# Fused attention and two expert layers: a batch's values in six tiles, loaded once

## The chip, the cores and the metric

One core of one Trainium2 chip runs the whole program. The metric is the time on the device in microseconds (us); the median over several executions counts. One further execution was recorded by the profiler, and every duration below comes from that one.

## The reference, cut to what matters

```python
def _attn_ref(q, k, v, w_pre, w_post):          # q, k, v: [2, 12, 448, 64]
    scores = (1 / 8) * q @ k^T                  # per batch and head, [448, 448]
    scores = einsum('bhij,hg->bgij', scores, w_pre)     # mix over the 12 heads
    attn = softmax(scores, axis=-1)
    attn = einsum('bhij,hg->bgij', attn, w_post)        # mix over the heads again
    return attn @ v
def reference(...):
    x = attention as [896, 768]
    x = (h * clip(h + 3, 0, 6) / 6) @ w_out     with h = x @ w_in     # first expert layer, d_ff 2048
    return (P(h) / Q(h)) @ w_out2               with h = x @ w_in2    # second expert layer
```

## The kernel before, in words

The attention works on eight chunks of query rows, numbered 0 to 7: four for each batch, with 120, 120, 120 and 88 rows. Chunks 0 to 3 belong to the first batch, 4 to 7 to the second. A chunk is worked through in steps of 20 rows: six steps in a chunk of 120 rows, five in one of 88.

What happens to a chunk is spread over three turns of the main loop (L503 to L569); turn 3 is the one in which chunk 3 is premixed, chunk 4's scores are made and spread, and chunk 2's result is multiplied with the values. One turn early, `scores` multiplies queries and keys for it (TensorE, tile `sc`, L225), the results are copied to a staging tile, and the head mix needs them in another layout: partitions must run over (row, head). So `spread` (L197) sends each head's scores with two DMAs into the tile `full`, one on SP's queue and one on GpSimd's, 24 DMAs for a chunk. Chunks 0 and 1 use `spread_group` (L203) in the same way, by groups of rows from one staging tile. In its own turn, each step does `premix` (tile `M`, L245, which reads `full`), the maximum on VectorE (L251), the exponential on ScalarE (L253), `norm` (L263 on GpSimd makes the weights `wr`), and two steps later `postmix` (tile `A`, L287) and its copy to `at` (L295). One turn later, `av_unit` multiplies `at` with the values (tile `X`, L310) in six units of two heads each, laid into steps 3 to 5 by the table `AVST`; at the last step of a turn comes a unit for head pair 4 and 5, and then the next turn begins with `premix` of the next chunk.

All engines execute in the order in which the code is written (a manual schedule). SP's queue carries nearly all loads, and it is one row: queries (`load_q`, tile `qraw`), keys (`load_k`), values (`load_v`, tile `vraw`), SP's half of the spreads, and the first weights of the expert layers (`load_unit`, tile `wraw`).

The values of a batch are six loads of 240 KB, one for each pair of heads. Before the change the tile `vraw` has four buffers. Each `av_unit` (L302) ends with `load_v` (L314) for the head pair four places further on, round and round through the chunks, so the six loads of a batch are issued again for every one of its chunks; each load waits for the `av_unit` that last read its buffer. The last chunk takes its values from one larger tile, `vlast` (`load_vs`, L130), in a buffer of `full`. The first four loads are issued in turn 0, step 1 (L521).

Of the kernel before, what the change touches and what calls it, by code (L numbers as in the profile page):

```python
# [7 lines left out]
F32 = mybir.dt.float32  # L8
# [11 lines left out]
B, H, S, D = 2, 12, 448, 64  # L20
JP, JC, JH = 120, 4, 56
# [5 lines left out]
NCH = 4  # L27
MG = CH // GR
NP = H // 2


def plan():

    chunks = []
    for b in range(B):
        for c in range(NCH):
            n = min(CH, S - c * CH)
            chunks.append((b, c * CH, n, 2 * ((n + 2 * GR - 1) // (2 * GR))))
    return chunks
# [7 lines left out]
def fused_kernel(  # L47
# [15 lines left out]
    nc = tc.nc  # L63
# [7 lines left out]
    chunks = plan()  # L71
    pairs = [(C, g) for C, c in enumerate(chunks) for g in range(0, c[3], 2)]

# [22 lines left out]
    att = tc.alloc_tile_pool(name="att", bufs=2)  # L96
# [14 lines left out]
    vraw = {}  # L111

    def load_q(C):
        ns = chunks[C][3] * GR
        t = front.tile([128, NP, CH], F32, tag="qraw", bufs=3, name=f"qraw{C}")
        nc.sync.dma_start(out=t[:, :, :ns], in_=q[C, :, :, :ns])
        qraw[C] = t

    def load_k(b, hp):
        if hp == 0:  # L120
            keys[b] = front.tile([128, NP, S], F32, tag="keys", bufs=2, name=f"keys{b}")
        nc.sync.dma_start(out=keys[b][:, hp], in_=k[b, :, hp])

    def load_v(C, hp):
        if C < len(chunks) - 1:
            t = att.tile([JP, 2, JC * D], F32, tag="vraw", bufs=4, name=f"vraw{C}_{hp}")
            nc.sync.dma_start(out=t, in_=v[chunks[C][0], hp])
            vraw[(C, hp)] = t

    def load_vs():  # L130

        C = len(chunks) - 1
        t = att.tile([JP, NP, 2, JC * D], F32, tag="full", bufs=2, name="vlast")
        for hp in range(NP):
            nc.sync.dma_start(out=t[:, hp], in_=v[chunks[C][0], hp])
            vraw[(C, hp)] = t[:, hp]


    BF16 = mybir.dt.bfloat16
# [11 lines left out]
    for i, w in enumerate((w_pre, w_post)):  # L151
        for a in range(0, 128, 64):
            nc.sync.dma_start(
                out=wrep[a : a + HP, i, :], in_=w[None, :, :].to_broadcast([HR, H, H])
            )
    load_q(1)
    load_q(2)
    nc.scalar.preload_act_table_set("natural_log_exp_and_others")
    nc.gpsimd.memset(mask2, 1.0)
    nc.gpsimd.affine_select(out=mask2, in_=mask2, pattern=[[-64, 2], [-H, HR]], compare_op=ALU.is_ge,  # L160
# [10 lines left out]
    def load_ab():  # L171
        nc.sync.dma_start(out=pa, in_=p_a.partition_broadcast(128))
        nc.sync.dma_start(out=pb, in_=p_b.partition_broadcast(128))

    def build_ab():
        nc.scalar.activation(out=pb, in_=pb, func=AF.Abs)
        nc.vector.tensor_scalar(out=pa, in0=pa, scalar1=-1.0, scalar2=None, op0=ALU.mult)
# [17 lines left out]
    full = {}  # L195
# [7 lines left out]
    def spread_group(C, g, st):  # L203
        n = chunks[C][3]
        for a, eng in enumerate((nc.sync, nc.gpsimd)):
            eng.dma_start(
                out=full[C][64 * a : 64 * a + HP, g, :],
                in_=st[a * HR * n : (a + 1) * HR * n].rearrange("(i g) h s -> g i (h s)", g=n)[g],
            )
# [64 lines left out]
    def postmix(m):  # L274
        C, g = pairs[m]
        if g == 0:
            at[C] = att.tile([JP, JC, H, CH], F32, tag="at", bufs=2, name=f"at{C}")
        e, st = epx.pop(m)
        wr = wrs.pop(m)
        av = A[:, :, : JC * H * GR].rearrange("p r (c h i) -> p r c h i", c=JC, h=H)  # L280
        for jc in range(JC):
            for a in range(2):
                for r in range(2):
                    o = slice(64 * r, 64 * r + HP)
                    for c in range(2):
                        j = (2 * jc + c) * JH
                        nc.tensor.matmul(  # L287
                            av[64 * c : 64 * c + JH, r, jc, :, a * HR : a * HR + HR],
                            lhsT=e[o, a, j : j + JH], rhs=wr[o, a], start=True, stop=True,
                        )  # L290
# [11 lines left out]
    def av_unit(C, h, tag="sc"):  # L302
        b, r0, n, G = chunks[C]
        if h % 4 == 1:
            xps[C] = ps.tile([128, 512], F32, tag=tag, bufs=BUFS[tag], name=f"X{C}_{h}")
        X = xps[C][:, : 2 * CH].rearrange("p (h n) -> p h n", n=CH)
        for jc in range(JC):
            for hh in (h - 1, h):
                vs = vraw[(C, hh // 2)][:, hh % 2, :].rearrange("p (c d) -> p c d", d=D)
                nc.tensor.matmul(  # L310
                    X[hh % 2 * D : hh % 2 * D + D, hh % 4 // 2, :n], lhsT=vs[:, jc, :], rhs=at[C][:, jc, hh, :n],
                    start=(jc == 0), stop=(jc == JC - 1),
                )
        load_v(*((C, h // 2 + 4) if h // 2 + 4 < NP else (C + 1, h // 2 + 4 - NP)))  # L314
        if h % 4 == 1:
            return []
        c0 = (h - 3) // 2
        t0 = b * S + r0
        src = X[:, :, :n]
        cs, ts_ = slice(c0, c0 + 2), slice(t0, t0 + n)  # L320
        o = XH[:, cs, ts_]
        return [
            lambda: nc.scalar.activation(out=o, in_=src, func=AF.Copy),
            lambda: nc.vector.tensor_tensor(out=XL[:, cs, ts_], in0=src, in1=o.bitcast(F32), op=ALU.subtract),
        ]
# [168 lines left out]
    PRE, LATE = B * NCH - 2, 4  # L494
# [3 lines left out]
    def pieces(n):  # L498
        for _ in range(n):
            next(wpieces, None)  # L500

    m = 0
    for C, (b, r0, n, G) in enumerate(chunks):  # L503
        nxt = C + 1 if C + 1 < len(chunks) else None
        G //= 2
        for s in range(G):
            if C and C + 2 < len(chunks) and s == (3 if C == 1 else 0):
                load_q(C + 2)
            if C == 0 and s == 3:
                for g in range(chunks[1][3]):  # L510
                    spread_group(1, g, stage1)
                XL = xp.tile([128, KD, NT], F32R, tag="xl", name="xl")
            if C == 2 and s >= 3:
                load_k(1, 2 * s - 6)
                load_k(1, 2 * s - 5)
            if C == 2 and s == 1:
                load_ab()
            if C == 3 and s == 0:
                build_ab()
            premix(m)  # L520
            if C == 0 and s == 1:  # L521
                for i in range(4):
                    load_v(0, i)
            for p in later:
                p()
            later.clear()
            sc, xs = [], []
            if m >= LAG:
                postmix(m - LAG)
            if nxt is not None and not C:  # L530
                if s < NP - FIRST:
                    sc += scores(nxt, FIRST + s, st=stage1[:, 2 * FIRST + 2 * s : 2 * FIRST + 2 * s + 2])
            elif nxt is not None:
                for hp in range(NP):
                    if SST[hp] == s:
                        sc += scores(nxt, hp)
            if C:
                for i, t in enumerate(AVST[G] if nxt is not None else AVLAST):
                    if t == s:
                        xs += av_unit(C - 1, 2 * i + 1)  # L540
            for p in sc[:-1]:
                p(vcopy)
            if m >= LAG:
                at_evac(m - LAG, acopy)
            for p in sc[-1:]:
                p(acopy)
            for p in xs[::2]:
                p()
            later += xs[1::2]
            norm(m)  # L550
            if C == PRE and s == LATE - 1:
                front.release()
                pools["late"] = tc.alloc_tile_pool(name="late", bufs=1, side="right", reuse_waits="tile")
                load_units(1)
                wpieces = (p for u in units[:4] for p in split_pieces(u))
            if C == PRE and s == G - 1:
                pieces(1)
            if C > PRE:
                pieces(2)
            if C > PRE and s == 1:  # L560
                load_vs()
            if C > PRE and s == 2:
                load_units(2)
            if nxt is None and s >= 3:
                if s == 3:
                    h100 = gemm1(0, 0, ps.tile([128, 512], F32, tag="sc", bufs=BUFS["sc"], name="h1_0_0"))
                for _ in range(3):
                    next(h100)
            m += 1  # L569

    C = len(chunks) - 1
# [77 lines left out]
    for c in range(KD):  # L649
        hp = [bank(f"y1_{c}_{p}") for p in range(2)]  # L650
# [77 lines left out]
    for f in range(KF):  # L728
# [10 lines left out]
        hp = hps[0]  # L739
# [5 lines left out]
        if f == 0:  # L745
            hp = hps[1]
            run(gemms[1])
        else:
            hp = bank2(tags[1], f"h2_{f}_1")
# [62 lines left out]
    for i in range(KF - TAIL):  # L812
        with tc.issue_after(last[0].ins), tc.issue_after(last[1].ins):
            if i + 2 >= AHEAD:
                prep(i + 2)
            if i < len(late_f):
                f = late_f[i]
# [4 lines left out]
    for t in range(NB1):  # L822
        row = P0 + t * TB
        o = gp.tile([TB, DM], F32, tag="o", bufs=3, name=f"o1_{t}")
        for j in range(2):
            for i in range(KF - TAIL, KF):
                f = order[i]
# [59 lines left out]
```

## Time and profile before

| | |
|---|---|
| median of 3 runs | 725.79 us (725.75 to 730.34) |
| the profiled execution | 725.2 us |
| its span, first to last instruction | 723.4 us |
| TensorE (PE) busy | 663.3 us, 92% |
| VectorE (DVE) busy | 502.5 us, 69% |
| ScalarE (ACT) busy | 383.4 us, 53% |
| GpSimd (POOL) busy | 88.6 us, 12% |
| packets moved by DMA | 124.42 MB |

The span is what the views divide up; the 1.8 us between it and the profiled execution's own time lie outside the first and last instruction. The attention takes the first 257 us of it, the two expert layers the rest. The profile's "released by" columns name the engine or the transfer whose completion ended a wait. A busy TensorE may run at either of two clock rates; the column PEclk gives the granted one as a share of 2.4 GHz.

### The profile page before, as it was taken

The numbers are of one execution on the slowest core, as the hardware profiler recorded it, in microseconds if no ns is written. First come the engines' busy times: TensorE is split into PE (matmuls) and PEld (weight loads), VectorE is DVE, ScalarE is ACT, GpSimd is POOL, SyncE is SP. The second block draws the span as 40 slices with busy tenths as digits, with TensorE's granted clock in tenths as the row PEclk, the third lists the DMA queues.
The fourth block names the chain that finished last, engine by engine and source line by source line (L and its number), as shares of the span: only waits on it lengthen the run. The fifth ranks groups of instructions, "written<-read, shape, count | busy, mean of one in ns | idle before, by whom it ended". The sixth has DMA issues, their size and how long they took to land.

```text
span 723.4 us, 16553 instructions
## 1 busy us (share of the span) xinstructions
PE 663.3 (92%) x6682; PEld 555.0 (77%) x6682; DVE 502.5 (69%) x860; ACT 383.4 (53%) x701; POOL 88.6 (12%) x163
## 2 busy tenths in 40 slices
PE   8875968668696999999999999999999999999997
PEld 2444655445564788989888888889999999999997
DVE  4443526345274569989888666537999899989991
ACT  3544537254464544655544323315767667679851
POOL 4342405133241510000000000000000000000000
PEclk9888889788899999999999999999999999999999
DMA  6666485565549457676654423344675764665522
GB/s 199 171 151 170 133 201 153 143 165 129 146 129 257 131 165 219 199 216 197 203 162 158 141 93 116 104 180 151 220 260 180 260 223 169 220 218 196 175 88 88
DMA packets 78737, 124.42 MB, mean 172 GB/s; under 512 B 12084, under 2 KB 57148, under 8 KB 78660
## 3 DMA queue, kind: packets, MB, share of 16 engines
q1 hardware_dynamic: 70692, 113.04, 49.2%
q0 software_dynamic: 7680, 9.95, 6.3%
q8 instruction: 53, 0.87, 0.5%
q10 hardware_dynamic: 288, 0.37, 0.1%
q14 instruction: 24, 0.20, 0.1%
HBM read 84.24 MB, written 19.27 MB: 143 GB/s over the span
## 4 chain that ended last, share of the span: by engine, by line
PE 84%; DMA 9%; issue 3%; ACT 1%; SPq 1%; POOL 1%; DVE 1%; POOLq 0%; ACTq 0%; DVEq 0%
PE h L331 11%; PE h L332 11%; PE h L333 11%; DMA vraw<-in_v_dram 6%; PE y L331 5%; PE y L333 5%; PE acc L331 5%; PE acc L332 5%; PE acc L333 5%; PE y L332 5%; PE X L310 5%; PE M L245 5%; PE sc L225 5%; PE A L287 4%; DMA full<-stage 2%
## 5 line engine op out<-in xcount | busy, mean ns | idle before, releaser
L331 PE MATMUL h<-xh,wh 128*128 128x512 f32 (+1 forms) x384 | 140.3, 365 | 0.0
L332 PE MATMUL h<-xl,wh 128*128 128x512 f32 (+1 forms) x384 | 140.1, 365 | 0.0
L333 PE MATMUL h<-xh,wl 128*128 128x512 f32 (+1 forms) x384 | 139.1, 362 | 0.0
L251 DVE TENSOR_REDUCE st<-M 128x1 f32<-128x448 f32 x92 | 53.2, 619 | 92.8 <-PE M L245 92.0
L253 ACT ACTIVATE e<-M,st 128x448 f32<-128x448 f32 x92 | 57.5, 629 | 60.3 <-DVE st L251 60.3
L310 PE MATMUL X<-at,vraw 120*64 120x120 f32 (+1 forms) x672 | 46.4, 302 | 41.0 <-DMA vraw<-in_v_dram 41.0
L331 PEld LDWEIGHTS h<-xh,wh 128*128 128x128 f32 x384 | 72.1, 188 | 8.2 <-POOL wr L263 0.2
L333 PEld LDWEIGHTS h<-xh,wl 128*128 128x128 f32 x384 | 72.1, 188 | 8.1
L287 PEld LDWEIGHTS A<-wr,e 60*56 60x56 f32 x2944 | 50.9, 133 | 34.7 <-issue 24.6
L332 PEld LDWEIGHTS h<-xl,wh 128*128 128x128 f32 x384 | 72.2, 188 | 6.6
L379 ACT ACTIVATE wf<-wraw 128x768 f32<-128x768 f32 (+1 forms) x56 | 49.5, 884 | 48.8 <-DVE wl L407 46.0
L310 PEld LDWEIGHTS X<-at,vraw 120*64 120x64 f32 x672 | 41.2, 160 | 43.0 <-issue 41.3
L406 ACT ACTIVATE wh<-wf 128x768 fp32r<-128x768 f32 (+1 forms) x52 | 42.6, 818 | 56.5 <-PE y L332 44.1
L333 PE MATMUL y<-gh,wl 128*128 128x384 f32 x192 | 70.6, 368 | 0.0
L331 PE MATMUL y<-gh,wh 128*128 128x384 f32 x192 | 70.5, 367 | 0.0
L407 DVE TENSOR_TENSOR wl<-wf,wh 128x768 fp32r<-128x768 f32 (+1 forms) x52 | 48.0, 924 | 31.8 <-ACT wh L406 31.8
L332 PE MATMUL y<-gl,wh 128*128 128x384 f32 x192 | 69.9, 364 | 0.0
L245 PE MATMUL M<-full,wp 60*64 60x448 f32 x368 | 56.5, 621 | 6.2 <-ACT e L253 3.2
L287 PE MATMUL A<-wr,e 60*56 60x60 f32 x2944 | 52.7, 220 | 7.1 <-POOL wr L263 4.7
L383 DVE SCALAR_TENSOR_TENSOR wf<-wraw,icst,wf 128x768 int32<-128x768 int32 (+1 forms) x56 | 55.2, 987 | 1.0
L387 DVE SCALAR_TENSOR_TENSOR wf<-wraw,icst,wf 128x768 int32<-128x768 int32 (+1 forms) x56 | 55.2, 986 | 0.7
L201 POOL DMA_DIRECT2D full<-stg x72 | 42.4, 589 | 83.9 <-DVE stg L230 52.7
(98 smaller groups left out, 1205.4 us busy)
## 6 DMA issues: line engine op xcount, KB each, us to landing
wraw<-in_moe_w_out_dram SPq DMA_DIRECT2D x28, 768.0 KB
wraw<-in_moe_w_in_dram SPq DMA_DIRECT2D x22, 768.0 KB
vraw<-in_v_dram SPq DMA_DIRECT2D x42, 240.0 KB
wpre<-in_moe_w_in_dram SPq DMA_DIRECT2D x10, 768.0 KB
w2h<-wh SPq DMA_DIRECT2D x16, 384.0 KB
w2l<-wl SPq DMA_DIRECT2D x16, 384.0 KB
ws<-w2h SPq DMA_DIRECT2D x16, 384.0 KB
ws<-w2l SPq DMA_DIRECT2D x16, 384.0 KB
```

Source lines behind the costliest of these rows:

```text
L245: nc.tensor.matmul(mt[a][64 * c : 64 * c + 64, :S], lhsT=wp[o], rhs=full[C][o, g + c, :], start=True, stop=True)
L251: nc.vector.tensor_reduce(out=st[:, a : a + 1], in_=mt[a][:, :S], op=ALU.max, axis=AX.X, negate=True)
L253: nc.scalar.activation(out=e[:, a], in_=mt[a][:, :S], func=AF.Exp, bias=st[:, a : a + 1], accum_out=st[:, 2 + a : 3 + a])
L287: nc.tensor.matmul(av[64 * c : 64 * c + JH, r, jc, :, a * HR : a * HR + HR], lhsT=e[o, a, j : j + JH], rhs=wr[o, a], start=True, stop=True,)
L310: nc.tensor.matmul(X[hh % 2 * D : hh % 2 * D + D, hh % 4 // 2, :n], lhsT=vs[:, jc, :], rhs=at[C][:, jc, hh, :n], start=(jc == 0), stop=(jc ...
L331: nc.tensor.matmul(o, lhsT=wh, rhs=mh, start=first, stop=False)
L332: nc.tensor.matmul(o, lhsT=wh, rhs=ml, start=False, stop=False)
L333: nc.tensor.matmul(o, lhsT=wl, rhs=mh, start=False, stop=last)
L379: nc.scalar.activation(out=w, in_=hw.bitcast(F32), func=AF.Copy, scale=2.0**-112)
L383: nc.vector.scalar_tensor_tensor(out=wi, in0=hw, scalar=icst[:, 0:1], in1=wi, op0=ALU.bitwise_and, op1=ALU.bitwise_or)
L387: nc.vector.scalar_tensor_tensor(out=wi, in0=lw, scalar=icst[:, 1:2], in1=wi, op0=ALU.logical_shift_right, op1=ALU.bitwise_or)
L407: nc.vector.tensor_tensor(out=lv, in0=w, in1=hv.bitcast(F32), op=ALU.subtract)
```

## The change

The tile `vraw` gets six buffers instead of four, and a batch's six loads are issued once: the first batch's in turn 0 (two each in steps 2, 4 and 5), the second batch's in turn 4, each behind the `av_unit` that is the last to read the same buffer for the first batch. `load_vs` and its tile go. The load of chunk 2's queries, which stood among the first loads of the program, moves to turn 0, step 1, behind the spreads of chunk 0.

```diff
-    def load_v(C, hp):
-        if C < len(chunks) - 1:
-            t = att.tile([JP, 2, JC * D], F32, tag="vraw", bufs=4, name=f"vraw{C}_{hp}")
-            nc.sync.dma_start(out=t, in_=v[chunks[C][0], hp])
-            vraw[(C, hp)] = t
-
-    def load_vs():
...
+    def load_v(b, hp):
+        vraw[(b, hp)] = att.tile([JP, 2, JC * D], F32, tag="vraw", bufs=NP, name=f"vraw{b}_{hp}")
+        nc.sync.dma_start(out=vraw[(b, hp)], in_=v[b, hp])
...
     load_q(1)
-    load_q(2)
...
-                vs = vraw[(C, hh // 2)][:, hh % 2, :].rearrange("p (c d) -> p c d", d=D)
+                vs = vraw[(b, hh // 2)][:, hh % 2, :].rearrange("p (c d) -> p c d", d=D)
...
-        load_v(*((C, h // 2 + 4) if h // 2 + 4 < NP else (C + 1, h // 2 + 4 - NP)))
+        if C == NCH - 1:
+            load_v(1, h // 2)
...
             if C == 0 and s == 1:
-                for i in range(4):
-                    load_v(0, i)
+                load_q(2)
+            if C == 0 and s in (2, 4, 5):
+                for i in range(2):
+                    load_v(0, (0, 0, 0, 0, 2, 4)[s] + i)
...
-            if C > PRE and s == 1:
-                load_vs()
```

On SP's queue, around turn 0, there stands before (`qraw` queries of chunks 1 and 2, the first `full` the spreads of chunk 0, the second those of chunk 1, the third those of chunk 2):

```order
L116 DMA qraw_150<-in_q_dram 128x720
L116 DMA qraw_152<-in_q_dram 128x720
L206 DMA full_169<-stage 60x1x448 x12
L127 DMA vraw_0_291<-in_v_dram 120x512
L127 DMA vraw_1_293<-in_v_dram 120x512
L127 DMA vraw_2_295<-in_v_dram 120x512
L127 DMA vraw_3_297<-in_v_dram 120x512
L206 DMA full_233<-stage_125 60x1x448 x12
L201 DMA full_581<-stg_0_584 5x12x448 x2
```

And now, in the same place:

```order
L116 DMA qraw_150<-in_q_dram 128x720
L195 DMA full_167<-stage 60x1x448 x12
L116 DMA qraw_289<-in_q_dram 128x720
L126 DMA vraw_0_313<-in_v_dram 120x512
L126 DMA vraw_1_315<-in_v_dram 120x512
L195 DMA full_231<-stage_125 60x1x448 x12
L126 DMA vraw_2_447<-in_v_dram 120x512
L126 DMA vraw_3_449<-in_v_dram 120x512
L126 DMA vraw_4_500<-in_v_dram 120x512
L126 DMA vraw_5_502<-in_v_dram 120x512
L190 DMA full_585<-stg_0_588 5x12x448 x2
```

The queries of chunk 2 and two values loads now stand ahead of chunk 1's spreads in the place of four values loads, and four values loads stand ahead of chunk 2's spreads, where none stood.

On SP's queue, from the end of chunk 4's spreads (`full_1460`) to the start of chunk 5's (`full_1844`), there stands before:

```order
L201 DMA full_1460<-stg_5_1611 5x12x448 x2
L127 DMA vraw_4_1684<-in_v_dram 120x512
L127 DMA vraw_5_1694<-in_v_dram 120x512
L127 DMA vraw_0_1705<-in_v_dram 120x512
L127 DMA vraw_1_1766<-in_v_dram 120x512
L127 DMA vraw_2_1777<-in_v_dram 120x512
L127 DMA vraw_3_1787<-in_v_dram 120x512
L116 DMA qraw_1796<-in_q_dram 128x720
L201 DMA full_1844<-stg_0_1847 5x12x448 x2
```

And now, with the same two spreads under the names `full_1440` and `full_1812`:

```order
L190 DMA full_1440<-stg_4_1586 5x12x448 x2
L190 DMA full_1440<-stg_5_1591 5x12x448 x2
L116 DMA qraw_1764<-in_q_dram 128x720
L190 DMA full_1812<-stg_0_1815 5x12x448 x2
L190 DMA full_1812<-stg_1_1820 5x12x448 x2
```

The six values loads between the two spreads are gone, and the load of chunk 6's queries follows the spreads of turn 3 directly. Behind the spreads of the other turns now stand: in turn 1 the queries of chunks 3 and 4, in turn 2 the keys of the second batch and the queries of chunk 5, in turn 4 still six values loads and the queries of chunk 7, in turn 5 nothing, in turn 6 the first weights.

On PE, at the last unit of turn 2 and the first premix of chunk 3, with what each waits for (DMAHW are completions of SP's transfers, DMASW of GpSimd's), there stands before:

```order
L310 MATMUL X_9_1384<-at_692,vraw_4_1245 64x120 [waits DMAHW6_49,DVE_49]
L310 MATMUL X_9_1384<-at_692,vraw_4_1245 64x120 x7
L310 MATMUL X_9_1384<-at_692,vraw_5_1255 64x120 [waits DMAHW7_49]
L310 MATMUL X_9_1384<-at_692,vraw_5_1255 64x120 x7
L245 MATMUL M_0_1415<-full_1016,wp 64x448 [waits DMAHW3_49,DMAHW2_49,DMAHW4_49,DMAHW1_49,DMAHW5_49,DMAHW0_49,Activation_49]
```

And now:

```order
L299 MATMUL X_9_1368<-at_696,vraw_4_500 64x120 [waits DVE_49]
L299 MATMUL X_9_1368<-at_696,vraw_4_500 64x120 x7
L299 MATMUL X_9_1368<-at_696,vraw_5_502 64x120 x8
L234 MATMUL M_0_1395<-full_1008,wp 64x448 [waits DMAHW4_49,DMAHW3_49,DMAHW5_49,DMAHW2_49,DMAHW6_49,DMAHW1_49,DMAHW7_49,DMAHW0_49,Activation_49]
```

The unit no longer waits for a transfer; the premix behind it still waits for all of SP's spreads.

## Rows read from the trace of the kernel before

**Rows 1.** Who waited for whom on PE, 56 to 257 us: total, times, longest.

```profile
PE X L310 <- DMA vraw<-in_v_dram: 41.0, 7, 9.1
```

**Rows 2.** Busy time by stretch: length, PE, PEld, DVE, ACT, POOL; PEclk, DMA share, GB/s.

```profile
130.00:133.00 3.00, 0.17 (x2) 0.20 (x4) 0.00 (x0) 0.00 (x0) 0.00 (x0) 0.50 0.73 173
280.00:372.00 92.00, 92.00 (x458) 82.49 (x457) 85.54 (x122) 51.91 (x82) 0.00 (x0) 1.00 0.65 202
```

**Rows 3.** Timeline of PE, end of turn 3: start, length, instruction, [idle before, releaser].

```profile
123.60 1.04 PE L310 MATMUL X<-at,vraw 120*64 120x120 f32 x16
132.83 3.47 PE L310 MATMUL X<-at,vraw 120*64 120x120 f32 x32 [8.19 <-DMA vraw<-in_v_dram]
136.23 1.77 PE L245 MATMUL M<-full,wp 60*64 60x448 f32 x8
137.78 1.20 PE L287 MATMUL A<-wr,e 60*56 60x60 f32 x64
138.91 1.42 PE L225 MATMUL sc<-keys,qraw 64*120 64x448 f32 x5
```

**Rows 4.** Timeline of SP's queue, the same turn.

```profile
110.06 15.31 SPq L201 DMA_DIRECT2D full<-stg  x12
125.46 11.20 SPq L127 DMA_DIRECT2D vraw<-in_v_dram  x6
```

**Rows 5.** DMA view, windows 128:130, 131:131.5, 70.6:71.1, 163:164, 192.5:193.2, in this order.

```profile
DMA packets 272, 0.47 MB, mean 237 GB/s; under 512 B 30, under 2 KB 116, under 8 KB 272
...
DMA packets 56, 0.11 MB, mean 225 GB/s; under 512 B 1, under 2 KB 1, under 8 KB 56
...
DMA packets 64, 0.06 MB, mean 116 GB/s; under 512 B 44, under 2 KB 44, under 8 KB 64
...
DMA packets 50, 0.09 MB, mean 92 GB/s; under 512 B 5, under 2 KB 6, under 8 KB 50
...
DMA packets 104, 0.19 MB, mean 269 GB/s; under 512 B 12, under 2 KB 14, under 8 KB 104
```

**Rows 6.** DMA view, window 46:48: packets, and SP's queue with its share.

```profile
DMA packets 148, 0.24 MB, mean 122 GB/s; under 512 B 12, under 2 KB 148, under 8 KB 148
...
q1 hardware_dynamic: 148, 0.24, 33.4%
```

**Rows 7.** Timeline of PE at the ends of turns 1, 2, 4, 5 and 6.

```profile
73.33 3.46 PE L310 MATMUL X<-at,vraw 120*64 120x120 f32 x32 [9.07 <-DMA vraw<-in_v_dram]
76.73 0.98 PE L245 MATMUL M<-full,wp 60*64 60x448 f32 x8
...
95.56 1.02 PE L287 MATMUL A<-wr,e 60*56 60x60 f32 x64
102.44 3.47 PE L310 MATMUL X<-at,vraw 120*64 120x120 f32 x32 [5.86 <-DMA vraw<-in_v_dram]
105.83 1.75 PE L245 MATMUL M<-full,wp 60*64 60x448 f32 x8
...
167.42 1.68 PE L245 MATMUL M<-full,wp 60*64 60x448 f32 x8
...
185.57 1.86 PE L310 MATMUL X<-at,vraw 120*64 120x120 f32 x32
...
194.54 3.47 PE L310 MATMUL X<-at,vraw 120*64 120x120 f32 x32 [4.46 <-DMA vraw<-in_v_dram]
197.94 1.77 PE L245 MATMUL M<-full,wp 60*64 60x448 f32 x8
...
222.84 2.89 PE L310 MATMUL X<-at,vraw 120*64 120x120 f32 x32 [4.49 <-DMA vraw<-in_v_dram]
225.65 1.58 PE L245 MATMUL M<-full,wp 60*64 60x448 f32 x8
```

**Rows 8.** Timeline of SP's queue, turn 1: the first nine spreads of chunk 2.

```profile
47.45 11.98 SPq L201 DMA_DIRECT2D full<-stg  x9
```

**Rows 9.** Timeline of PE, end of turn 0.

```profile
40.64 1.86 PE L287 MATMUL A<-wr,e 60*56 60x60 f32 x64 [4.29 <-POOL wr L263]
```

More of the change, by code (lines that the diff above doesn't have):

```diff
@@ L122, in load_k @@
         nc.sync.dma_start(out=keys[b][:, hp], in_=k[b, :, hp])
-    def load_v(C, hp):
-        if C < len(chunks) - 1:
-            t = att.tile([JP, 2, JC * D], F32, tag="vraw", bufs=4, name=f"vraw{C}_{hp}")
-            nc.sync.dma_start(out=t, in_=v[chunks[C][0], hp])
-            vraw[(C, hp)] = t
-    def load_vs():
[L132 to L136, printed above, removed]
+    def load_v(b, hp):
+        vraw[(b, hp)] = att.tile([JP, 2, JC * D], F32, tag="vraw", bufs=NP, name=f"vraw{b}_{hp}")
+        nc.sync.dma_start(out=vraw[(b, hp)], in_=v[b, hp])
     BF16 = mybir.dt.bfloat16
```

## The prediction

> **What bounds the kernel now.** I read the waits of PE first, because PE is busy for most of the span. In the attention they name one cause that stands out: the value multiplications (X) wait for the values' loads, 41.0 us in seven waits, the longest 9.1 [rows 1]. Behind the attention PE is busy without a gap, 92.00 of 92 us [rows 2], so whatever the attention saves should reach the end nearly whole.
>
> Then the timeline of PE at the end of a turn. Turn 3 shows the pattern: a first unit at 123.60, then 8.19 us of nothing, the last unit at 132.83, and at 136.23 the premix M of the next chunk [rows 3]. The last unit runs at half rate: 3.47 us against 1.86 for the same 32 multiplications elsewhere [rows 3, 7]; the granted clock around its start is 0.50, the 1.2 GHz level, after PE stood still [rows 2].
>
> The third view is SP's queue in the same turn, since the loads come from there: twelve spreads from 110.06 to 125.4, and only then the six values loads [rows 4]. The loads are late because the spreads are in front of them. So I ask when the spreads themselves land, for M needs all of them. SP's spreads move rows of 448 floats, 1792 bytes, the only packets in these windows between 512 bytes and 2 KB. In 128:130 there are 116 - 30 = 86 of them, in 131:131.5 none [rows 5]. The last one passes at about 131.0, and X starts 1.8 us later. In the same way the last spread packet is gone before 70.6 in turn 1, passes about 163.2 in turn 4 (6 - 5 = 1 is left) and about 192.7 in turn 5 (14 - 12 = 2) [rows 5]. That is the heart of the forecast: take the loads away, and the next wait, M on its spreads, ends only 4 to 5 us before M starts today.
>
> **The change part by part.** Gone are 36 loads of 240 KB: 42 + 6 before, 12 now. No engine computes less. What it is worth I work out at the six entries into a new chunk. M can start when PE has done the last unit, or when the spreads have landed, whichever is later. For landing I add 0.7 us to the last packet. The rows do not show this; it lies between 0 and 1.8 us, the time from the last spread packet to X at 132.83, when values were still arriving. I take 0.7 because values packets fill a good part of those 1.8.
>
> Behind the spreads fewer packets now follow. With SP's spreads alone 148 - 12 = 136 of their packets pass in 2 us, in 128:130 beside the values 86 [rows 5, 6]; for some 120 packets left at 128 that is 1.4 us. I take all of it where nothing follows (turn 5), half where one or two loads of queries follow (turns 1 and 3), none where six values loads or the weights still do (turns 4 and 6).
>
> Into chunk 2: 70.6 + 0.7 - 0.7 = 70.6, but four values loads (983 KB) now stand ahead of the spreads on SP. The spreads cannot absorb this: nine issues take 11.98 us [rows 8], so the queue is backed up. At 237 GB/s [rows 5] they cost 4.1 us, at the 122 GB/s of the spreads alone [rows 6] 8.1; below, nothing, if they fill gaps. I take 4.1, since a load of this kind is spread wider than a spread. The queries that leave the first loads are 360 KB, 0 to 1.6 us at 237 GB/s; they run beside the scores, so I take 0.5. M at 74.2 instead of 76.73 [rows 7]: 2.5.
>
> Into chunk 3: PE stopped at 102.44 - 5.86 = 96.58, and the unit takes 1.86: ready at 98.4. The spreads of a 100-row chunk are shorter, but the keys follow them; I allow 0.5. 98.9 instead of 105.83 [rows 7]: 6.9.
>
> Into chunk 4: 131.0 + 0.7 - 0.7 = 131.0 instead of 136.23 [rows 3]: 5.2. PE would be ready at 124.64 + 1.86 = 126.5, so 4.5 us of waiting stay.
>
> Into chunk 5: 163.2 + 0.7 = 163.9 instead of 167.42 [rows 7]: 3.5.
>
> Into chunk 6: 192.7 + 0.7 - 1.4 = 192.0; PE is ready at 194.54 - 4.46 + 1.86 = 191.9. Instead of 197.94 [rows 7]: 5.9.
>
> Into chunk 7: weight packets hide the spreads in the DMA view. In turn 3 X started 1.1 us after the landing (132.83 - 131.7); so 222.84 - 1.1 = 221.7 instead of 225.65 [rows 7]: 4.0.
>
> Together 28.0. The small seventh wait, in the last turn, I count as nothing.
>
> Against this stands the clock. The half rate behind a wait now falls on M and the postmix A instead of on X. Into chunk 2, M goes from 0.98 to 1.77 [rows 3, 7] and A from 1.02 to 1.86, its length behind the 4.29 us wait of turn 0 [rows 7, 9]: 1.6 lost. Into chunks 4 and 5, M is slow today already and A goes from 1.20 to 1.86: 0.7 each. Where the wait goes, into chunks 3 and 6, M gains 0.8 each. Net 1.4 lost.
>
> So 28.0 - 1.4 = 26.6. The profiled execution took 725.2 us, 1.8 more than its span; 725.2 - 26.6 = 698.6. The median shown is 0.6 above that execution, so I say 699.
>
> Other edits cost nothing that I can find. The second batch's loads wait for their buffers' last readers in turn 4, but are first needed a turn later. Chunk 2's queries are needed only in the turn after their new place. The weights move up on SP past two values loads; should ScalarE still have to wait for them, that is at the entry into chunk 7, where I have taken off nothing for it.
>
> **A rule weighed.** In 46:48, with SP's queue alone, it holds 33.4% of 16 engines, 5.3 of them, at 122 GB/s [rows 6]. The Trainium skill, "DMA: Bandwidth & Descriptors", section "Why a DMA increments its semaphore by 16 and not by 1", says that a transfer is split over the largest number up to 16 that divides the outermost size on both sides, and from SP always over the lowest-numbered engines. That would be five for the spreads here, which agrees with the 33.4%, and it speaks against the change: values loads issued later can only queue behind the spreads on those five, so removing them would shorten no tail, and the sum would be 2.8 us smaller. The 86 packets against 136 [rows 5, 6] say that the tail does slow down, so I keep the 2.8.
>
> **The rivals.** First, PE becomes the bound and the spreads are in time everywhere: 41.0 goes, and with it the half rate of five units (four at 1.6, one at 1.0) [rows 3, 7] and of four M (0.8 each): 725.2 - 41.0 - 7.4 - 3.2 = 674. For it speaks that DMA has less to do; against it that nothing competes with the middle of a turn's spreads today, as the values loads come behind them [rows 4].
>
> Second, no difference that counts: DMA used the pauses, and the spreads stretch until M starts when it starts today. Only the entry into chunk 3, where PE itself is the bound, keeps its 6.9 - 1.4 = 5.5: 720. For it: even in 130:133, with PE still, DMA's share is 0.73 [rows 2]. Against: from 131.0 on there were no spreads left to move.
>
> Third, slower: the four values loads ahead of chunk 2's spreads pass one after the other instead of together. At the longest wait for a load, 9.1 us [rows 1], they cost 36.4. Without my 4.1 the rest gains 30.7: 725.2 - 30.7 + 36.4 = 731. It decides from 30.7 / 4 = 7.7 us a load. For it speaks the backed-up queue [rows 8], against it that six loads issue within 11.20 us today [rows 4].
>
> **How the numbers follow.** The forecast has 0.82, PE as the bound 0.10, no difference 0.06, slower 0.02. A measurement of this kernel can tell about 1% from no change, 7 us. So faster 0.92, within 1% 0.06, slower 0.02. For the range, on the good side the four loads cost nothing (4.1), the tails of turns 1, 3 and 4 clear up whole (0.7 + 0.7 + 1.4), the landing takes 0.2 instead of 0.7 at the four entries bound by it (2.0) and the clock costs nothing (1.4): 10.3, so 688, and I reach on to 684 towards the first rival. On the bad side the loads cost 8.1 (4.0 more), no tail gets shorter (2.8), and landing takes 1.8 at five entries (5.5): 12.3, so 711; I say 712.
>
> **What would show it.** In the profile after, PE's waits for the values are gone, and in their place M waits for the spreads, into chunk 4 about 4.5 us, into 5 about 6, into 2 about 8, and hardly into 3 and 6. M of chunk 7 starts near 199 on the span. Behind a wait M lasts 1.7 and A 1.9. GEMM stretches keep their length. It is wrong if M does not wait at all (first rival), if the spreads' last packets come as long after the first as the turn lasts today (second), or if M into chunk 2 starts after 76.7 (third, or 8.1 for the loads).

## The result, and the profile after

| | before | after |
|---|---|---|
| median (lowest to highest), same chip | 727.58 us (725.75 to 730.34) | 707.24 us (705.19 to 710.75) |
| ratio, 95% interval | | 0.9722 [0.9665, 0.978] |
| the profiled execution | 725.2 us | 706.1 us |
| its span | 723.4 us | 704.4 us |
| packets moved by DMA | 124.42 MB | 115.57 MB |

Faster by 20.3 us, between the medians. The forecast was 699, in a range from 684 to 712. So the sign is right, and of the 26.6 us of the sum some 6 to 8 did not come.

The waits of PE in the attention of the changed kernel (total, times, longest), beside [rows 1]:

```profile
PE M L234 <- DMA full<-stg: 8.2, 2, 7.0
PE M L234 <- ACT e L242: 8.0, 1, 8.0
PE M L234 <- DMA vraw<-in_v_dram: 7.8, 1, 7.8
PE A L276 <- issue: 3.1, 2, 2.3
```

The 41.0 us of X behind the values are gone whole, and M waits in their place. The third row names the values, though M reads none; the profile puts a wait down to what landed last before its end. The row of 8.0 for ScalarE is in no part of the prediction. The expert layers are as full as before [rows 2], in a stretch of the same length (length, PE, PEld, DVE, ACT, POOL; PEclk, DMA share, GB/s):

```profile
258.00:350.00 92.00, 92.00 (x457) 82.39 (x457) 84.52 (x121) 51.12 (x80) 0.00 (x0) 1.00 0.65 199
```

From M of chunk 7 to the end of the span it is 497.0 us (704.4 - 207.41), before 497.8 (723.4 - 225.65). So what was gained in the attention reached the end, and the turns are where to look. The timeline of PE in the changed kernel, at the entries into chunks 1 to 7, for [rows 3, 7]; the second line stands in the middle of turn 1:

```profile
40.98 1.73 PE L234 MATMUL M<-full,wp 60*64 60x448 f32 x8
...
65.41 2.38 PE L234 MATMUL M<-full,wp 60*64 60x448 f32 x8 [7.96 <-ACT e L242]
...
75.93 1.04 PE L234 MATMUL M<-full,wp 60*64 60x448 f32 x6 [1.20 <-DMA full<-stg]
...
99.11 1.04 PE L234 MATMUL M<-full,wp 60*64 60x448 f32 x6 [0.52 <-ACT at L284]
...
101.30 1.77 PE L214 MATMUL sc<-keys,qraw 64*120 64x448 f32 x8
...
125.78 2.20 PE L234 MATMUL M<-full,wp 60*64 60x448 f32 x8 [6.97 <-DMA full<-stg]
127.30 2.28 PE L276 MATMUL A<-wr,e 60*56 60x60 f32 x64
129.51 2.38 PE L214 MATMUL sc<-keys,qraw 64*120 64x448 f32 x8
...
157.32 2.20 PE L234 MATMUL M<-full,wp 60*64 60x448 f32 x8 [7.81 <-DMA vraw<-in_v_dram]
158.84 2.28 PE L276 MATMUL A<-wr,e 60*56 60x60 f32 x64
...
183.66 1.04 PE L234 MATMUL M<-full,wp 60*64 60x448 f32 x6 [2.28 <-issue]
...
207.41 1.04 PE L234 MATMUL M<-full,wp 60*64 60x448 f32 x6
```

Subtract the starts of M from one another, and the same in [rows 3, 7]. A turn is the time between two of them:

| | before | after | gained | forecast (clock left out) |
|---|---|---|---|---|
| start to chunk 2 | 76.73 | 75.93 | 0.8 | 2.5 |
| turn 2 | 29.10 | 23.18 | 5.9 | 6.9 |
| turn 3 | 30.40 | 26.67 | 3.7 | 5.2 |
| turn 4 | 31.19 | 31.54 | -0.3 | 3.5 |
| turn 5 | 30.52 | 26.34 | 4.2 | 5.9 |
| turn 6 | 27.71 | 23.75 | 4.0 | 4.0 |

The rows add up to 18.3, of 19.0 us of span. Turn 4, in which the second batch's six loads still come, is furthest below its forecast. The other place to look is turn 1, which has four values loads ahead of its spreads. Both in SP's queue (for [rows 4, 8]):

```profile
43.51 4.41 SPq L126 DMA_DIRECT2D vraw<-in_v_dram  x4
48.63 18.54 SPq L190 DMA_DIRECT2D full<-stg  x12
...
103.00 13.73 SPq L190 DMA_DIRECT2D full<-stg  x12
...
131.82 16.30 SPq L190 DMA_DIRECT2D full<-stg  x12
148.22 6.22 SPq L126 DMA_DIRECT2D vraw<-in_v_dram  x6
```

The twelve issues behind the four loads take 18.54 us, in turn 3 13.73. That explains the wait of 7.96 for ScalarE. VectorE's copy of the sixth pair of heads into its staging tile found all five buffers still being read by spreads; it stood still for 9.09 us, and the maxima and exponentials of the turn are queued behind that copy:

```profile
63.10 0.62 DVE L219 COPY stg<-sc 120x448 f32<-120x448 f32 x1 [9.09 <-DMA full<-stg]
```

Last, the DMA view at the end of turn 3, windows 122:124 and 124.6:125.7 (for [rows 5, 6]):

```profile
DMA packets 136, 0.24 MB, mean 121 GB/s; under 512 B 10, under 2 KB 122, under 8 KB 136
...
q1 hardware_dynamic: 136, 0.24, 32.6%
...
DMA packets 14, 0.03 MB, mean 26 GB/s; under 512 B 4, under 2 KB 4, under 8 KB 14
```

122 - 10 = 112 packets of spreads pass in the first window, none in the second. The last one passes at 124.3, and M starts at 125.78, 1.5 us behind it. In 122:124 no queue but SP's moves anything, and the engines' time is two thirds idle.

### The profile page after: what moved, and what is told of

Read it like the earlier page. It is cut to its first block, busy times and chain, and to the rows that moved or that the text cites. A ratio compares the mean times of both kernels' runs of the same rounds, so it can differ in the third digit from the quotient of the medians.

```text
span 704.4 us, 16483 instructions
## 1 busy us (share of the span) xinstructions
PE 657.6 (93%) x6682; PEld 552.3 (78%) x6682; DVE 502.7 (71%) x860; ACT 383.3 (54%) x701; POOL 88.7 (13%) x163
## 2 busy tenths in 40 slices
DMA packets 73876, 115.57 MB, mean 164 GB/s; under 512 B 11544, under 2 KB 56608, under 8 KB 73800
## 4 chain that ended last, share of the span: by engine, by line
PE 83%; DMA 11%; ACT 2%; DVE 2%; issue 1%; POOL 1%; SPq 0%; DVEq 0%; POOLq 0%; ACTq 0%
PE h L321 11%; PE h L322 11%; PE h L323 11%; DMA full<-stg 8%; PE y L321 6%; PE y L323 6%; PE acc L321 6%; PE acc L323 6%; PE acc L322 6%; PE y L322 6%; PE sc L214 5%; PE M L234 5%; PE A L276 4%; PE X L299 3%; DMA full<-stage 2%
## 5 line engine op out<-in xcount | busy, mean ns | idle before, releaser
L234 PE MATMUL M<-full,wp 60*64 60x448 f32 x368 | 57.5, 602 | 29.6 <-ACT e L242 8.5
L276 PEld LDWEIGHTS A<-wr,e 60*56 60x56 f32 x2944 | 54.0, 136 | 34.4 <-issue 22.5
L323 PE MATMUL y<-gh,wl 128*128 128x384 f32 x192 | 70.6, 368 | 0.0
L276 PE MATMUL A<-wr,e 60*56 60x60 f32 x2944 | 56.0, 225 | 10.5 <-POOL wr L252 5.9
L234 PEld LDWEIGHTS M<-full,wp 60*64 60x64 f32 x368 | 14.1, 139 | 53.1 <-issue 23.7
L190 POOL DMA_DIRECT2D full<-stg x72 | 42.4, 589 | 71.1 <-DVE stg L219 53.0
L284 ACT COPY at<-A 120x960 f32<-120x960 f32 x46 | 44.9, 975 | 9.3 <-PE A L276 9.3
```

Source lines behind the costliest of these rows:

```text
L234: nc.tensor.matmul(mt[a][64 * c : 64 * c + 64, :S], lhsT=wp[o], rhs=full[C][o, g + c, :], start=True, stop=True)
L276: nc.tensor.matmul(av[64 * c : 64 * c + JH, r, jc, :, a * HR : a * HR + HR], lhsT=e[o, a, j : j + JH], rhs=wr[o, a], start=True, stop=True,)
L284: copy(out=at[C].rearrange("p c h n -> p (c h) n")[:, :, c0 : c0 + 2 * GR].rearrange("p x (r i) -> p r x i", r=2), in_=A[:JP, :, : JC * H ...
L323: nc.tensor.matmul(o, lhsT=wl, rhs=mh, start=False, stop=last)
```

## The experiments

Theory: the changed kernel waits for its spreads; values loads delay them where they share a turn. Rivals: the staging buffers, the place of a load in the queue, SP's queue, GpSimd's work, and all transfers together. Each run is given as its ratio to the kernel before, run on the same chip.

**How far a profile can be trusted.** The changed kernel once more.

> The changed kernel once more, to see how far the stretches between the chunks differ between two profiles of the same program. Theory: the lengths of the turns differ by 1 us or less between the two profiles, so that differences of 3 us and more in other runs are their own. Rival: the transfers' times vary from run to run by 2 us and more in a turn, as the turns of the runs so far suggest (M into chunk 2 at 74.5, 75.9 and 80.3 in three programs that are the same up to there).

709.88 us (705.45 to 712.34), ratio 0.9764 [0.9694, 0.9833]. Its timeline of PE, entries into chunks 2, 4 and 5:

```profile
78.75 1.04 PE L234 MATMUL M<-full,wp 60*64 60x448 f32 x6 [1.48 <-DMA qraw<-in_q_dram]
...
129.98 1.76 PE L234 MATMUL M<-full,wp 60*64 60x448 f32 x6 [5.95 <-DMA full<-stg]
...
159.72 1.13 PE L234 MATMUL M<-full,wp 60*64 60x448 f32 x6 [4.36 <-DMA vraw<-in_v_dram]
```

At chunk 4 it is 4.2 us behind the other execution, and turn 4 took 29.7 us instead of 31.5: gained 1.5 instead of -0.3. Its six rows of the table would read -2.0, 4.1, 4.2, 1.5, 4.1 and 3.2, and all gains are counted from one profile of the kernel before. The turns of these two profiles differ by up to 1.8 us. Two programs below that are the same up to chunk 2 enter it at 74.47 and 80.28, with turns 1 of 34.2 and 38.1 us. So a single turn of a single profile is good to about 2 us, turn 1 to about 4, and medians to about 3.

**The four loads ahead of chunk 2's spreads.** One kernel leaves them out:

```diff
-            if C == 0 and s in (2, 4, 5):
-                    load_v(0, (0, 0, 0, 0, 2, 4)[s] + i)
+            if C == 0 and s == 2:
+                    load_v(0, i)
+                for hp in range(2, NP):
+                    vraw[(0, hp)] = vraw[(0, hp % 2)]
```

> The first batch's values are loaded for the first two pairs of heads only and used for all six (the other pairs' values are left out), so that no values load stands ahead of the spreads of chunk 2. Theory, that the four loads cost what the prediction put at 4.1 us and more, by way of the staging buffers: M into chunk 2 comes 4 to 7 us earlier than 75.9, at 69 to 72, and no wait is left in the middle of turn 1. Rival, that the loads are nearly free there: at 74 or later.

In its one run it takes 709.93 us. Its PE and, below, SP's queue in turn 1:

```profile
42.28 1.73 PE L234 MATMUL M<-full,wp 60*64 60x448 f32 x8
...
71.47 2.20 PE L234 MATMUL M<-full,wp 60*64 60x448 f32 x8 [5.88 <-DMA qraw<-in_q_dram]
```

```profile
47.04 13.44 SPq L190 DMA_DIRECT2D full<-stg  x12
```

Turn 1 takes 71.47 - 42.28 = 29.2 us; with the loads 75.93 - 40.98 = 35.0, and 78.75 - 43.12 = 35.6 in the second profile of the changed kernel. The twelve issues take 13.44 instead of 18.54, and the wait in the middle of the turn is gone. By this run the four loads cost about 6 us. The whole is no faster than the changed kernel: 4.5 us ahead of its first profile at chunk 2, it is 2.7 ahead at chunk 6 (180.99) and 0.6 behind at chunk 7 (208.00). Turns of the same instructions took the lead back; why they were longer in this execution stays open.

The second kernel issues all six loads ahead of chunk 1's spreads:

```diff
-            if C == 0 and s in (2, 4, 5):
-                for i in range(2):
-                    load_v(0, (0, 0, 0, 0, 2, 4)[s] + i)
+            if C == 0 and s == 2:
+                for i in range(NP):
+                    load_v(0, i)
```

> All six values loads of the first batch are issued in turn 0, step 2, ahead of chunk 1's spreads; none stands ahead of chunk 2's. Theory, that the price of a load is the time of its transfer, wherever spreads are queued behind it: turn 0 gets 3 to 5 us longer (M of chunk 1 at 44 to 46 instead of 41), turn 1 as much shorter, M into chunk 2 within 2 us of 75.9, the whole within 2 us. Rival, that the place ahead of chunk 2's spreads is the bad one, because of the staging buffers: M into chunk 2 at 71 to 73 and the whole 3 to 5 us faster.

707.12 us (705.42 to 709.28), ratio 0.9734 [0.9674, 0.9794]: no difference. Its entries into chunks 1 and 2:

```profile
45.28 2.18 PE L234 MATMUL M<-full,wp 60*64 60x448 f32 x5
...
76.88 1.10 PE L234 MATMUL M<-full,wp 60*64 60x448 f32 x6
```

Turn 1, without the four loads here too, shrinks to 31.6 us, which puts their price at 3.4 to 4.0 us. But M of chunk 1 comes at 45.28 instead of 40.98 (43.12 in the second profile): the price moved along with the loads.

**The staging buffers.** Is the wait of 9.09 us a cause?

```diff
-            st = front.tile([CH, 2, S], F32, tag="raw", bufs=5, name=f"stg{C}_{hp}")
+            st = front.tile([CH, 2, S], F32, tag="raw", bufs=6, name=f"stg{C}_{hp}")
```

> Six staging buffers for a chunk's head pairs instead of five, everything else as in the changed kernel. Theory: the wait of 8 us in the middle of turn 1 is the copy of the sixth pair, which waits for a staging buffer until the first pair's spread has landed; the spreads are late because four values loads stand ahead of them on SP. With six buffers the copy does not wait, the 8 us in the middle go, but M into chunk 2 still waits for the spreads, whose end is set by the transfers: it moves from 75.9 by less than 2 us, and the whole gains 0 to 3. Rival, that the buffer itself is the cause (late copies make late spreads): M into chunk 2 comes 4 us or more earlier, and the whole gains 4 or more.

712.12 us (708.65 to 713.84), ratio 0.976 [0.9728, 0.9792]: not faster. PE now waits once, at the end of the turn:

```profile
79.01 1.76 PE L234 MATMUL M<-full,wp 60*64 60x448 f32 x6 [12.53 <-DMA full<-stg]
```

The buffer only decided where in the turn the wait stood. The spreads end no earlier: M of chunk 2 is 3.1 us later than in the first profile and 0.3 later than in the second.

**The second batch's loads in turn 4.** Left out:

```diff
-            load_v(1, h // 2)
+            vraw[(1, h // 2)] = vraw[(0, h // 2)]
```

> The second batch's values are not loaded; its chunks use those of the first batch (left out: six loads in turn 4). Theory, that these loads slow the end of the spreads of turn 4: the stretch from M of chunk 4 to M of chunk 5 falls from 31.5 us to 28 to 29.5. Rival, that they cost nothing there: 31 to 31.5.

In its one run it takes 714.39 us. Entries into chunks 4 and 5:

```profile
133.71 2.27 PE L234 MATMUL M<-full,wp 60*64 60x448 f32 x8 [5.25 <-issue]
...
161.10 1.76 PE L234 MATMUL M<-full,wp 60*64 60x448 f32 x6 [4.05 <-DMA full<-stg]
```

Turn 4 takes 27.4 us, against 31.5 and 29.7 with the loads in the two profiles of the changed kernel, and 28.4 in the run with six loads early. But this is not the loads' price alone. SP's queue in turn 4, here and then in the second profile:

```profile
138.99 13.68 SPq L190 DMA_DIRECT2D full<-stg  x12
```

```profile
135.21 14.35 SPq L190 DMA_DIRECT2D full<-stg  x12
149.65 7.33 SPq L126 DMA_DIRECT2D vraw<-in_v_dram  x6
```

The first values load is issued behind the last spread, and by then the twelve issues have taken 13.68 us here, 14.35 in the second profile and 16.30 in the first. Loads that are not yet issued can't have made that difference. From the end of the last issue to M of chunk 5 it is 8.4 us here (161.10 - 152.67) and 9.2 and 10.2 in the two profiles, but 6.3 with the loads in the run with six loads early (157.22 - 150.87). A price of 1 to 2 us behind the spreads is possible, and not shown. Moved into turn 5, behind its first premix:

```diff
+        if b == 1 and hp == 0:
+            nc.vector.memset(vraw[(b, hp)][:, 0, 0:1], 0.0)
...
-            load_v(1, h // 2)
...
+            if C == NCH + 1 and s == 0:
+                for hp in range(NP):
+                    load_v(1, hp)
```

> The second batch's six values loads are issued in turn 5, behind the first premix of that turn (VectorE writes one element of the first tile there, and SP's loads wait for it), instead of behind the spreads of turn 4. My theory is that in turn 4 these loads slow the last spreads and their completion: then M of chunk 5 comes earlier, the stretch from M of chunk 4 to M of chunk 5 falls from 31.5 us to 28 to 29.5, and the whole gains 2 to 3 us, since the transfers now fall into the time in which no spreads move. Rival, that this stretch is long because its turn begins at half clock and has six steps, and the loads behind the spreads cost nothing: 31 to 31.5 us, and the loads, now ahead of the spreads of turn 5, add up to 2 us to that turn.

710.25 us (706.52 to 715.39), ratio 0.9732 [0.968, 0.9784]. Entries into 5 and 6, and the middle of turn 5:

```profile
154.54 1.04 PE L236 MATMUL M<-full,wp 60*64 60x448 f32 x6 [1.84 <-DMA full<-stg]
174.28 2.37 PE L236 MATMUL M<-full,wp 60*64 60x448 f32 x8 [4.76 <-ACT e L244]
184.16 1.06 PE L236 MATMUL M<-full,wp 60*64 60x448 f32 x6 [0.58 <-ACT at L286]
```

SP's issues of turn 4 in this run:

```profile
130.89 15.85 SPq L192 DMA_DIRECT2D full<-stg  x12
```

Turn 4 is 154.54 - 124.63 = 29.9 without any values load in it, as long as with them in the second profile: the theory's 28 to 29.5 was missed. Turn 5 is 29.6 instead of 26.3 and 26.4, with the wait in mid-turn that the four loads make in turn 1. So ahead of the spreads six loads cost about 3 us, and behind them nothing that these two runs can show.

**The queries of chunk 2** back among the first loads:

```diff
+    load_q(2)
...
-            if C == 0 and s == 1:
-                load_q(2)
```

> Only the move of chunk 2's queries is undone: they are loaded among the first loads again. The prediction gave the move 0.5 us, with bounds 0 and 1.6; theory: M of chunk 1 starts 0 to 1.6 us later at its first transfers but has 360 KB less ahead of chunk 1's spreads, so the whole stays within 1 us of the changed kernel. Rival, that the move is what shortened turn 0 (M of chunk 1 at 40.3 to 42.3 instead of 42.3): M of chunk 1 comes at 42.3 or later, and the whole loses 1 to 2 us.

709.51 us (709.26 to 709.95), ratio 0.9766 [0.971, 0.9822]; M of chunk 1 starts at 39.47. This part of the change is worth nothing that can be measured.

**Is it SP's queue?** Every third head's SP spread is issued by GpSimd, so that GpSimd issues sixteen and SP eight:

```diff
-        for a, eng in enumerate((nc.sync, nc.gpsimd)):
+        for a, eng in enumerate((nc.gpsimd if h % 3 == 2 else nc.sync, nc.gpsimd)):
```

> Of the 12 spreads that SP issues in a turn, from chunk 2's on, four (every third head's) are issued by GpSimd instead, so that it has 16 and SP 8. Theory: what now ends last in a turn is SP's own twelve spreads, which use a third of the transfer engines only; with eight of them a turn's spreads land 3 to 5 us earlier, the waits of M for its spreads shrink, the whole gains 6 to 14 us over the changed kernel. Rival, that all transfers together are the limit whichever queue issues them: no gain, within 2 us. Second rival, that GpSimd becomes the bound, since the weights of the postmix wait in its queue behind the issues: A waits longer for them, and the kernel is slower by 3 us or more.

712.11 us (706.01 to 715.2), ratio 0.9773 [0.9686, 0.986]. No wait of M from chunk 2 on is put down to spreads any more (two in the first turns are, 2.8 us, and 2.6 us are put down to nothing that the profile shows), but the weights `wr`, which GpSimd computes, came late:

```profile
PE A L276 <- POOL wr L252: 19.7, 9, 4.5
```

So `wr` was given to VectorE (`nc.gpsimd.tensor_tensor` in `norm` becomes `nc.vector.tensor_tensor`), together with the sixteen spreads and, as a control, alone.

> Every third head's SP spread is issued by GpSimd (as in the run that moved only that), and the weights wr are made by VectorE in place of GpSimd, so that no computation stands behind GpSimd's spreads. Theory (SP's own twelve spreads a turn, some 22 to 25 us from the first scores, are what the turn waits for): the 19.7 us of A behind wr go, M's waits for spreads stay under 3 us in total, the stretch into chunk 4 falls from about 26.8 to 21 to 24 us, and the time is 693 to 702, 6 to 15 below the changed kernel. Rival (all transfers of a turn together are the bound, whichever queue issues them): the waits for spreads come back as GpSimd's share lands late, and the time is within 3 us of the changed kernel, 705 to 712.

> Control for the run beside it: only the weights wr move from GpSimd to VectorE, the spreads stay as in the changed kernel. Theory (spreads are the bound): M's waits for spreads and for the first scores stay, some 15 to 25 us in total, the waits of A for wr (5.9 us in two) go, which M's next wait takes up; 704 to 711, no difference from the changed kernel that can be measured. Rival (wr on GpSimd, queued behind the issue of spreads, holds the turns): 3 to 6 us faster by itself, 701 to 705.

With sixteen spreads 713.49 us (710.5 to 716.05), ratio 0.9791 [0.973, 0.9852]; `wr` alone 706.76 (704.6 to 711.51), ratio 0.969 [0.9625, 0.9755]. The theory lost: A no longer waits for `wr`, and yet the time is no better than with twelve and twelve. PE in turn 3, with sixteen spreads and then in the control:

```profile
107.65 1.77 PE L214 MATMUL sc<-keys,qraw 64*120 64x448 f32 x8
...
130.68 2.45 PE L234 MATMUL M<-full,wp 60*64 60x448 f32 x6 [5.22 <-DMA full<-stg]
```

```profile
107.47 1.77 PE L214 MATMUL sc<-keys,qraw 64*120 64x448 f32 x8
...
130.62 2.20 PE L234 MATMUL M<-full,wp 60*64 60x448 f32 x8 [5.44 <-DMA full<-stg]
```

From the turn's first scores to the next M are 23.0 us with sixteen and 23.2 in the control; in the changed kernel 125.78 - 101.30 = 24.5, and 23.8 in its second profile. Taking a third of SP's spreads away shortens nothing that can be told from the control. Even SP's own last spread packet passes 21.8 us after the first scores (at 129.4), with all twelve in the control 22.2 (at 129.6). The DMA view just before M with sixteen spreads (129:130.6) shows the other queue at the end:

```profile
q0 software_dynamic: 39, 0.04, 8.5%
q1 hardware_dynamic: 13, 0.03, 4.7%
```

GpSimd's packets (q0) now come last. The third queue, ScalarE's:

```diff
+        for a, eng in enumerate((nc.scalar if h % 3 == 2 else nc.sync, nc.gpsimd)):
```

> Every third head's SP spread is issued by ScalarE in place of SP, wr stays on GpSimd. Theory (SP's queue with its twelve spreads is the bound): M's waits for spreads fall under 5 us in total and A does not wait for wr beyond the 5.9 us of the changed kernel; ScalarE pays some 0.1 to 0.5 us an issue, four a turn; 695 to 704. Rival (all transfers together are the bound, or ScalarE stalls at its issues as SP does, 15 us for twelve): the exponentials come late, PE waits for e by 2 us a turn more, and the time is 707 to 720.

711.6 us (710.9 to 714.88), ratio 0.9775 [0.9717, 0.9833]. M's waits for spreads fall to 8.0 us over the whole span, from 18.3 in the changed kernel (8.2, the 7.8 that name the values, and 2.3 in the first turns). Other waits take their place:

```profile
PE A L276 <- ACT at L284: 25.9, 19, 3.8
PE A L276 <- POOL wr L252: 5.7, 2, 5.5
PE M L234 <- DMA full<-stg: 5.2, 2, 2.8
...
PE M L234 <- DMA full<-stage: 2.8, 2, 2.0
```

ScalarE spends 0.74 us on each issue, and its copies of A (`at`) stand behind them in its order; A, which has one buffer, waits for those copies 19 times. The Trainium skill, "DMA: Bandwidth & Descriptors", section "Why a DMA increments its semaphore by 16 and not by 1", lets transfers of the hardware queues always go over the lowest-numbered engines; by that ScalarE's spreads would share SP's five and free nothing. No view here names a packet's engine, so this stays the page's word.

Last, a smaller step: only every sixth head (`h % 6 == 5`), fourteen to ten, with `wr` on VectorE.

> As the run with sixteen spreads on GpSimd and wr on VectorE, but only every sixth head's SP spread moves: SP issues ten a turn, GpSimd fourteen. In the changed kernel SP's spreads run alone at the end of a turn, at 32.6% of the engines (136 packets in 122 to 124 us), some 4 us longer than GpSimd's. Theory (SP's end alone sets the turn): two spreads of 105 KB less at some 120 GB/s are 1.8 us a turn, in the five turns bound by spreads up to 9 us, less what the half rate keeps: 699 to 704. Rival (every spread that ends later on either queue is waited for, and packets of the two queues slow each other): within 3 us of the kernel with wr alone on VectorE (706.76), 704 to 710, and the last spread packets of turn 3 come no earlier after the first scores than 22 us.

705.68 us (700.94 to 711.86), ratio 0.9706 [0.9659, 0.9754]. It has the lowest median of all, but 1.1 us from the control and 1.6 from the changed kernel, with intervals that overlap nearly whole: inconclusive, and no version that can be said to beat the changed kernel. Its PE in turn 3, and SP's last packets there (DMA view, 120:122 and 122:124):

```profile
99.08 1.77 PE L214 MATMUL sc<-keys,qraw 64*120 64x448 f32 x8
...
122.38 2.20 PE L234 MATMUL M<-full,wp 60*64 60x448 f32 x8 [5.46 <-DMA qraw<-in_q_dram]
```

```profile
DMA packets 78, 0.16 MB, mean 81 GB/s; under 512 B 9, under 2 KB 42, under 8 KB 78
...
DMA packets 4, 0.02 MB, mean 11 GB/s; under 512 B 1, under 2 KB 1, under 8 KB 3
```

From first scores to M are 23.3 us, about as with a third of the spreads moved. The last spreads pass at about 121.3 (33 packets in the first window, none in the second), 22.2 us after the first scores, where the rival had put them. So the floor of some 23 to 24.5 us from first scores to M is not the length of one queue. Nor is it the staging buffers, since with six of them it is 23.45 (130.92 - 107.47). The runs fit the rival: what a turn waits for is the spreads of all queues together. What in it binds, GpSimd's share, the engines that the two share or the time from issue to landing, these runs leave open. A spread in a form that keeps the engines busy for more than a third of the time was not tried.

## Why the prediction was right, and where its sum was off

**Right.** The waits for values go whole, and the next to end is M on its spreads; the expert layers keep their length. M of chunk 3 waits 0.52, where hardly any wait was forecast (2.88 in the second profile, put down to the keys). Turn 6 gains the 4.0 that were forecast, and 3.2 in the second profile. The sum was too good all the same: M of chunk 7, forecast near 199, starts at 207.41 and 210.66, and the medians of 707.24 and 709.88 lie toward the bad end of the range.

**Turn 4** is the term furthest off in the table. "163.2 + 0.7", no change in the tail since the six loads still follow: 3.5 forecast, -0.3 and 1.5 measured. The step took over the landing of before as if it were fixed. It has three parts, and all three came out longer:

| | before | forecast | after, two profiles |
|---|---|---|---|
| M of chunk 4 to the first scores | 2.68 | 2.68 | 3.73, 3.53 |
| first scores to the last spread packet | 24.3 | 24.3 | 26.4, 24.9 |
| last spread packet to M of chunk 5 | 4.2 | 0.7 | 1.4, 1.3 |

The first is the clock, below. Why the second grew stays open. It can't be laid on the loads behind the spreads: it is 23.1 in the run without them (160.4 - 137.29, its first scores), but 25.4 in the run that moves them into turn 5 (153.8 - 128.36). The third is 0.7 in both of these runs, so the loads that follow may be what lengthens it.

**The price of the four loads.** "I take 4.1": by the two runs without them in turn 1 it is 3.4 to 6.4 (turns of 35.0 and 35.6 us against 31.6 and 29.2, one profile each), inside the bounds 0 and 8.1. Its form was wrong. I expected about 8 us of waiting at M of chunk 2; 7.96 came in mid-turn, through the staging buffers, and 1.20 at the entry. I had looked at SP's queue and not at who waits for the buffers that its transfers read. In the second profile M of chunk 2 starts at 78.75, beyond the 76.7 that I named as a sign that the loads cost more; of the 2.8 us behind the first profile, 2.1 come from a longer turn 0.

**The shorter tail,** 2.8 in all. In turn 3 it is not seen: from first scores to M 131.0 + 0.7 - 0.7 - 108.36 = 22.6 were forecast (before, the first scores of that turn start at 108.36); 24.5 and 23.8 were measured. In turn 5 the last spread packet passes 21.8 and 22.1 us after the first scores, before 22.7, so 0.6 to 0.9 of the 1.4 came. The 1.4 itself should have been 1.2: 120 packets at 136 in 2 us take 1.8 of the 3.0 us from 128 to 131.0 [rows 5, 6]. The rule that I had weighed and set aside came nearer in its sum, though by it the tail of turn 5 would have stayed as it was.

**The landing.** "I add 0.7": from the last spread packet to M it is 1.5 and 1.1 in turn 3, 1.4 and 1.3 in turn 4 and 0.9 in turn 5, where the rows allowed 0 to 1.8. The step was inside its bounds and too short at each of these entries.

**The clock.** M 1.7 and A 1.9 behind a wait were forecast. Behind waits of 7 us M takes 2.20 and A 2.28 at the lower of the two rates (granted clock 0.50, 1.2 GHz, in 125.7:129.5), and the next scores 2.38 instead of 1.77 with the clock rising under them (0.72 in 129.5:131.8). From M to the scores at the entry into chunk 4 are 3.73 us instead of 138.91 - 136.23 = 2.68 [rows 3]: 1.05 where I had 0.7, and another 0.6 at the scores.

**The rivals.** PE as the bound (674) fell with M's waits of 24 us. No difference (720): 707.24 lies below, though in turn 4 the spreads did stretch by 2.1 and 0.6 us, as its mechanism has it. Slower (731): the loads cost 3 to 6 us for four, not 9.1 each.

## What to carry to other kernels

When a wait for a load is taken away, ask when the next transfer in line lands, and take its time from its own start, not from where it ended beside the old traffic. A load that is issued once instead of every round still costs something in the turn in which it is left, where it stands ahead of the critical transfers; what it costs behind them these runs can't tell from nothing. Look for a turn with room. Before you lay a longer turn on a load, look whether the load had been issued when the time was lost, and take a second profile of the same program. A staging buffer that a slow transfer reads is a second way by which that transfer stops the engines; it shows as a wait of a copy, and of everything behind the copy.

## What the runs showed that was not expected

Two profiles of one program differ by 4.2 us at the entry into chunk 4 (125.78 and 129.98) and by 6.2 us in the end (706.1 and 712.34), with the same instructions; the time of transfers varies. And four ways to share a turn's spreads (SP twelve and GpSimd twelve, eight and sixteen, ten and fourteen, or four of SP's on ScalarE) give 707.24, 713.49, 705.68 and 711.6 us: nearly the same (with sixteen and fourteen, `wr` was on VectorE too), though in 122:124 of the changed kernel two thirds of the engines' time were idle.
